# Tile 0's values without half of the row copies, and a new order of the lead-in

## The chip, the cores and the metric

The kernel runs on one core of one Trainium2 chip. The metric is device time in microseconds (us) of one execution. A core has TensorE (PE in the profile, with PEld for its weight loads), VectorE (DVE), ScalarE (ACT), GpSimd (POOL) and SyncE (SP); each takes its own instructions strictly in the order in which the program gives them.

## The reference: what is computed

Causal attention in a window of 64 keys for 8 batches of 8 heads (576 positions, 64 dimensions a head), then a feed-forward layer with g = h * cos(h) on the 4608 rows:

```python
batch, n_heads, seq, head_dim = (8, 8, 576, 64)
...
scores = scale * np.matmul(q, k.transpose(0, 1, 3, 2))
mask = (rel >= 0) & (rel < window)              # window = 64
scores = np.where(mask, scores, -1000000000.0)
attn = np.exp(scores - max) / sum               # softmax by rows
attn_out = np.matmul(attn, v)                   # (B, H, S, D)
x = attn_out.transpose(0, 2, 1, 3).reshape(B * S, H * D)    # 4608 x 512
h = x @ w_in                                    # 512 -> 2048
g = h * np.cos(h)
out = g @ w_out                                 # 2048 -> 512
```

## The kernel before

**Tiles.** The 4608 rows of x are done in 9 tiles of 512 rows, `mt` 0 to 8. A tile's hidden layer has 16 blocks `ff` of 128 columns; each block is the sum of four matmuls, one for each pair of heads (`ks` or `p`, 0 to 3; `first`, L348), 64 matmuls in a tile. ACT then makes the sine, DVE the product gT, and PE the output rows from gT and `w_out` (L534). While a tile's feed-forward layer runs, the attention of the next batch runs in its gaps, by a plan of times (`at`, `pump`).

**Attention units.** A unit (b, p, j) is a batch, a pair of heads and 64 queries; its window is 128 keys, those of block j-1 and block j. Tile 0 needs 32 units, taken as 8 groups of four: group `p.g` has pair p and units 4g to 4g+3. For each group:

- `s` scores (PE, first a matmul that puts in the mask, then eight of 64x64), `m` maximum by rows (DVE), `e` exponentials with their sums (ACT, four), `i` reciprocal of the sums (DVE), `n` norm (POOL or DVE: weights w), `w` transpose on PE into a PSUM tile `tw_ps`, `c` copy of it to SBUF (`g_put`: DVE or ACT, tile wT).
- For each pair: `v` values (16 matmuls over 8 units and 2 heads into o_ps), `x` copy of o_ps to xT (`put_x`), the input of the hidden layer.

Before them stand `tq`, `tk` (transposes of the rows of q and k) and `pq`, `pk` (their copies out of PSUM, tile T).

**The values' rows.** V of batch 0 is loaded in chunks of 128 rows into slots 0, 2, 4, 6 of a tile with 8 slots (`values_of(0)`); the last 64 rows go into the lower half of slot 7 (`load_v`). A unit with odd j finds its 128 keys in slot j-1 as loaded. One with even j needs two halves of different chunks, so `spread_v` makes them: step `z.0` copies the lower 64 partitions of slots 2, 4, 6 to slots 1, 3, 5, and `z.1` the upper 64 partitions of slots 0, 2, 4, 6 to slots 1, 3, 5, 7. Then unit j finds its keys in slot j-1.

**The order of the lead-in.** All that happens before tile 0's hidden layer is written by hand in the string `FIRST`: each word is a step, with pair, group or half, and at the end the engine (a ACT, d DVE, p POOL). `h.p` are first hidden-layer matmuls, for pair p of the first blocks (`skewed`: blocks 0 to 2 before the change); `hx.ff` are those of block ff for pairs 0 and 1, `hl` the matmuls of pairs 2 and 3 of the skewed blocks (5 before the change), `tb` loads the sine's table on ACT. `l` issues the next of seven loads on POOL, in this order: three parts of w_in, q and k of batch 1, two halves of w_out. After `FIRST` POOL issues the last rows of v of batch 0 and the v of batch 1. SP issues only the first two loads in the lead-in.

**PSUM.** The banks O0, O1, X0, X1 and S are handed out by name (`H_FIRST` for the blocks of tile 0, `S_FIRST` for the scores of the lead-in); three more are taken in turn (`ps_t`, tag "t": the transposes and, before the change, all of tile 0's values). A tile waits until the one before it in its place has been read.

Of the kernel before, what the change touches and what calls it, by code (L numbers as in the profile page):

```python
# [10 lines left out]
def _safe_warn(msg, *a, **kw):  # L11
# [4 lines left out]
BF16 = mybir.dt.bfloat16  # L16
AF = mybir.ActivationFunctionType
ALU = mybir.AluOpType
# [7 lines left out]
GF = 4  # L26
# [9 lines left out]
SKEW = 3  # L36
# [3 lines left out]

FIRST = (
# [6 lines left out]
)  # L48


# [1 line left out]
def kernel(  # L52
# [9 lines left out]
    nc = tc.nc  # L62
    B, H, S, D = q.shape
    assert (B, H, S, D) == (8, 8, 576, 64)
    scale = 1.0 / math.sqrt(D)
    d_model = H * D
# [3 lines left out]
    TU = MT // 64  # L70
# [4 lines left out]
    att = ctx.enter_context(tc.tile_pool(name="att", bufs=3))  # L75
# [16 lines left out]
    st = {}  # L92

    H_FIRST = ("O1", "X0", "X1", "S", "O0") * 3 + ("X0",)
    H_SECOND = ("X0", "X1", "S", "O0", "O1") * 3 + ("t",)
    H_BANKS = ("X0", "O0", "X1", "S", "O1") * 2 + ("X0", "X1", "S", "O0", "O1", "t")
    S_BANKS = ("X1", "S", "X0")
# [3 lines left out]
    def bank(which, name):  # L103
        if which == "t":
            return ps_t.tile([128, 512], F32, tag="t", name=name)
        return ps.tile([128, 512], F32, tag=which, name=name)

    def copy(engine, out, in_):
        {"a": nc.scalar.copy, "p": nc.gpsimd.tensor_copy}.get(engine, nc.vector.tensor_copy)(out, in_)  # L109
# [46 lines left out]
    def values_of(b):  # L156
        return rowtiles[0][:, 0:8 * d_model].rearrange("p (s x) -> p s x", s=8) if b == B - 1 else vtiles[b % 3]

    def load_v(b, c):
        n = 128 if c < 4 else 64  # L160
        vt = values_of(b)[:n, 2 * c if c < 4 else 2 * c - 1]
        nc.gpsimd.dma_start(out=vt.rearrange("p (h d) -> p h d", h=H),  # L162
                            in_=v[b, :, c * 128:c * 128 + n, :].rearrange("h p d -> p h d"))


    def spread_v(b, half, engine="p"):
        vt = values_of(b)
        to, of = ((vt[0:64, 1:7:2], vt[0:64, 2:8:2]), (vt[64:128, 1:8:2], vt[64:128, 0:7:2]))[half]
        if engine == "dma":
            nc.sync.dma_start(out=to, in_=of)  # L170
        else:
            copy(engine, to, of)

    def load_w_in(lo, hi):
        nc.gpsimd.dma_start(out=w_in_sb[:, :, lo:hi], in_=w_in_v[:, :, lo:hi])
# [122 lines left out]
    def g_norm(n, engine="p"):  # L298
# [4 lines left out]
                                in1=rden[:, 0:u].unsqueeze(2).to_broadcast([128, u, 128]))  # L303
        st["w", n] = w

    def g_trans(n):
        w, u = st.pop(("w", n)), len(groups[n])
        if n in direct:
            st["tw", n] = t_ps = ps_t.tile([128, GF, 128], BF16, tag="t", name="tw_ps")
            for i in range(u):  # L310
                nc.tensor.transpose(t_ps[:, i], w[:, i], ident)  # L311
            return
        wT = att.tile([128, GF, 128], BF16, tag="wT", name="wT", bufs=20)
        nc.sync.dma_start(out=wT[:, 0:u], in_=w[:, 0:u].rearrange("p u c -> p (u c)"), transpose=True)
        st.update({("wT", unit): wT[:, i] for i, unit in enumerate(groups[n])})

    def g_put(n, engine=None):
        wT, u = att.tile([128, GF, 128], BF16, tag="wT", name="wT", bufs=20), len(groups[n])
        copy(engine, wT[:, 0:u], st.pop(("tw", n))[:, 0:u])
        st.update({("wT", unit): wT[:, i] for i, unit in enumerate(groups[n])})  # L320


    def values(mt, p):
        st["o", mt, p] = o_ps = bank("S", "o_ps") if mt > 1 and p == PAIRS - 1 else ps_t.tile([128, MT], F32, tag="t", name="o_ps")
        for i in range(TU):
            b, j = divmod(mt * TU + i, NU)
            wT = st["wT", (b, p, j)]
            cross = st["cross", (b, p, j)]
            for h in range(2):
                nc.tensor.matmul(out=o_ps[64 * h:64 * h + 64, 64 * i:64 * i + 64],  # L330
                                 lhsT=values_of(b)[:, max(j - 1, 0), 128 * p + 64 * h:128 * p + 64 * h + 64],
                                 rhs=wT[:, 64 * (h ^ cross):64 * (h ^ cross) + 64], start=True, stop=True, skip_group_check=True)


    def put_x(mt, p, engine=None):
        if ("xT", mt) not in st:
            st["xT", mt] = att.tile([128, PAIRS, MT], BF16, tag="xT", name="xT", bufs=2)
        o_ps = st.pop(("o", mt, p))
        copy(engine, st["xT", mt][:, p], o_ps)
# [8 lines left out]
    def first(mt, ff, ks, start, stop):  # L348
        if start:
            st["h", ff] = bank((H_FIRST, H_SECOND, H_BANKS)[min(mt, 2)][ff], "h_ps")  # L350
        nc.tensor.matmul(out=st["h", ff], lhsT=w_in_sb[:, ks, ff * 128:ff * 128 + 128],  # L351
                         rhs=st["xT", mt][:, ks], start=start, stop=stop)

    def skew(mt):
        return 5 if mt < 2 else SKEW

    def last_pairs(mt):
        for ff in range(skew(mt)):
            for ks in range(2, PAIRS):
                first(mt, ff, ks, False, ks == PAIRS - 1)  # L360

    def skewed(mt, ks, n):
        for ff in range(skew(mt) if mt else SKEW):
            first(mt, ff, ks, n == 0, n == PAIRS - 1)

    def last_rows(gT, o_sb):
# [27 lines left out]
    n = n_first  # L394
# [79 lines left out]
    def load():  # L474
# [6 lines left out]
             "pk": lambda p, engine="a": put("k", 0, p, engine),  # L481
             "mk": put_masks, "ck": lambda: cast("k", "d"), "l": load, "tb": sine_table, "h": lambda p: skewed(0, p, next(turn_h)), "hl": lambda: last_pairs(0),
             "hx": lambda ff: [first(0, ff, ks, ks == 0, False) for ks in range(2)],
             "z": lambda half, engine=None: spread_v(0, half, engine),
             "s": lambda p, g: g_scores(2 * p + g, next(turn_s) % 5), "m": lambda p, g: g_max(2 * p + g),
             "e": lambda p, g: g_exp(2 * p + g), "i": lambda p, g: g_inv(2 * p + g),
             "n": lambda p, g, engine: g_norm(2 * p + g, engine), "w": lambda p, g: g_trans(2 * p + g),
             "c": lambda p, g, engine=None: g_put(2 * p + g, engine), "v": lambda p: values(0, p),
             "x": lambda p, engine=None: put_x(0, p, engine)}
    for step in FIRST.split():  # L490
        name, *args = step.split(".")
        steps[name](*[int(a) if a.isdigit() else a for a in args])
    load_v(0, 4)
    for c in range(5):
        load_v(1, c)

    for mt in range(n_mt):
# [11 lines left out]
        for ff in range(n_ff):  # L509
# [8 lines left out]
            e = ff % 2  # L518
# [58 lines left out]
```

## Time and profile before

| what | before |
|---|---|
| median of 3 runs | 306.64 us (305.22 to 307.27) |
| profiled execution, its own time | 306.41 us |
| its span | 304.4 us |
| mean granted clock of TensorE | 0.993 |
| PE busy in the span | 288.7 us |
| DVE, ACT, POOL busy | 220.4, 235.7, 171.1 us |
| HBM read, written | 36.70 MB, 9.44 MB |

The span runs from the first to the last instruction in the trace. A row of the timeline gives start, duration, engine, line, operation, output and inputs, shape and count; in square brackets the idle time before it and what ended it. Durations of successive instructions of one engine overlap by some hundredths of a us, so what one costs is better read from the start of the next. The line of a copy is that of the helper `copy` (L109).

### The profile page before, as it was taken

Reading aid. Unit: us, or ns where it says so; the run is one execution under the profiler, and the core shown is the slowest. Engines: PE = TensorE matmul, PEld = TensorE weight load, DVE = VectorE, ACT = ScalarE, POOL = GpSimd, SP = SyncE. Lnnn points to the kernel's source line nnn. Section 1 sums busy time; section 2 is a strip of 40 time slices with the busy share of each in tenths; the row PEclk is TensorE's granted clock in tenths of the full one; section 3 lists DMA queues with packets and bytes.
Section 4 is the critical chain, followed back from the end, with each engine's and each line's share of the span. In section 5 each row is a group of like instructions: output and inputs, shape, how many; then the busy total and the mean of one; then the engine's idle time right before and its main releaser. Section 6 shows DMA issues by size and latency. Waiting matters only on the chain.

```text
span 304.4 us, 7847 instructions
## 1 busy us (share of the span) xinstructions
PE 288.7 (95%) x2628; PEld 142.1 (47%) x2668; DVE 220.4 (72%) x834; ACT 235.7 (77%) x786; POOL 171.1 (56%) x198
## 2 busy tenths in 40 slices
PE   3769999999999999999999999999999999999996
PEld 3544444544454445444544444444444454454443
DVE  3896889588787878787877787778778877236701
ACT  5997799967997799779987998799869986106600
POOL 8996257977774976497659665967433630000000
PEclk9989999999999999999999999999999999999999
DMA  7999999699969999999999979999994441011012
GB/s 150 181 211 207 207 155 139 105 165 191 225 114 155 225 164 132 154 201 183 138 167 208 189 106 172 157 219 123 180 172 110 87 130 62 0 72 70 0 69 71
DMA packets 165577, 43.88 MB, mean 144 GB/s; under 512 B 154720, under 2 KB 160800, under 8 KB 165536
## 3 DMA queue, kind: packets, MB, share of 16 engines
q0 software_dynamic: 99344, 18.06, 75.1%
q1 hardware_dynamic: 66048, 25.11, 40.2%
q8 instruction: 21, 0.34, 0.5%
q14 instruction: 20, 0.16, 0.2%
q10 hardware_dynamic: 144, 0.20, 0.2%
HBM read 36.70 MB, written 9.44 MB: 152 GB/s over the span
## 4 chain that ended last, share of the span: by engine, by line
PE 88%; DVE 6%; issue 2%; ACT 2%; DMA 1%; POOL 0%; DVEq 0%; POOLq 0%
PE h_ps L351 41%; PE out_ps L534 36%; PE o_ps L330 3%; PE s_ps L261 3%; DVE negm L273 1%; PE out_ps L371 1%; DMA first_f<-in_q_dram 1%; DVE w L302 1%; PE tq_ps L186 1%; DVE s L277 1%; DVE v L109 1%; PE tk_ps L186 1%; PE tw_ps L311 1%; PE s_ps L244 1%; ACT e L288 1%
## 5 line engine op out<-in xcount | busy, mean ns | idle before, releaser
L351 PE MATMUL h_ps<-xT,w_in 128*128 128x512 bf16 x556 | 127.1, 381 | 2.2 <-DVE xT L109 0.6
L534 PE MATMUL out_ps<-w_out,gT 128*128 128x512 bf16 x543 | 123.0, 379 | 1.8 <-issue 1.1
L522 DVE TENSOR_TENSOR gT<-h_ps,sin 128x512 bf16<-128x512 f32 x144 | 95.4, 688 | 33.6 <-ACT sin L519 33.4
L519 ACT ACTIVATE sin<-h_ps 128x512 f32<-128x512 f32 x144 | 82.9, 599 | 34.1 <-PE h_ps L351 32.8
L288 ACT ACTIVATE e<-s,negm 128x128 f32<-128x128 f32 x256 | 98.6, 388 | 0.3 <-DVE negm L277 0.3
L302 POOL TENSOR_TENSOR w<-e,rden 128x512 bf16<-128x512 f32 (+1 forms) x76 | 74.5, 993 | 31.5 <-DVE rden L295 29.1
L351 PEld LDWEIGHTS <-w_in 128*128 128x128 bf16 x576 | 56.0, 98 | 67.1 <-issue 2.7
L534 PEld LDWEIGHTS <-gT 128*128 128x128 bf16 x560 | 53.2, 98 | 62.4 <-issue 0.2
L277 DVE CUSTOM_DVE_ANT_0 s<-s_ps,mask 128x128 f32<-128x128 f32 x256 | 58.0, 284 | 0.1
L288 ACT ACTIVATION_READ_ACCUMULATOR e<-s,negm 128x1 f32 x256 | 48.1, 188 | 0.0
L149 POOL DMA_DIRECT2D rows<-in_q_dram x30 | 25.4, 867 | 25.9 <-DMA T<-rows 16.6
L162 POOL DMA_DIRECT2D v<-in_v_dram x35 | 29.8, 879 | 10.5 <-DMA rows<-in_k_dram 7.3
L109 ACT COPY out_sb<-out_ps 128x512 f32<-128x512 f32 (+1 forms) x18 | 10.1, 563 | 24.2 <-PE out_ps L534 18.7
L295 DVE RECIPROCAL rden<-den 128x4 f32<-128x4 f32 (+1 forms) x80 | 13.8, 172 | 19.2 <-ACT e L288 18.6
L149 POOL DMA_DIRECT2D rows<-in_k_dram x30 | 25.5, 897 | 2.2 <-DMA T<-rows 2.2
L109 DVE CAST xT<-o_ps 128x512 bf16<-128x512 f32 x27 | 17.6, 679 | 6.5 <-PE o_ps L330 6.3
L277 DVE DVE_READ_ACCUMULATOR2_ANT negm<- 128x1 f32 x256 | 21.2, 83 | 0.0
L109 DVE COPY out_sb<-out_ps 128x512 f32<-128x512 f32 x18 | 12.4, 689 | 12.0 <-PE out_ps L534 12.0
L288 ACT ACTIVATE e<-s_ps,negm 128x128 f32<-128x128 f32 x32 | 11.5, 425 | 1.6 <-DVE negm L273 1.6
L261 PE MATMUL s_ps<-T 64*64 64x128 bf16 x512 | 12.1, 221 | 0.0
L261 PEld LDWEIGHTS <-T 64*64 64x64 bf16 x512 | 8.2, 106 | 8.3 <-DVE negm L277 4.4
L330 PEld LDWEIGHTS <-v 128*64 128x64 bf16 x504 | 9.5, 112 | 4.3 <-issue 2.1
(56 smaller groups left out, 146.2 us busy)
## 6 DMA issues: line engine op xcount, KB each, us to landing
out_dram<-out_sb SPq DMA_DIRECT2D x16, 512.0 KB, 6.1
v<-in_v_dram POOLq DMA_DIRECT2D x28, 128.0 KB, 8.3
rows<-in_q_dram POOLq DMA_DIRECT2D x24, 128.0 KB, 5.2
rows<-in_k_dram POOLq DMA_DIRECT2D x24, 128.0 KB, 7.8
w_out<-in_moe_w_out_dram POOLq DMA_DIRECT2D x2, 1024.0 KB, 16.7
w_in<-in_moe_w_in_dram POOLq DMA_DIRECT2D x2, 768.0 KB, 12.4
wT<-w SPq DMA_TRANSPOSE x66, 3.9
out_dram<-out_sb SPq DMA_DIRECT2D x3, 256.0 KB, 2.0
```

The costliest lines, as they stand in the source:

```text
L109: {"a": nc.scalar.copy, "p": nc.gpsimd.tensor_copy}.get(engine, nc.vector.tensor_copy)(out, in_)
L149: nc.gpsimd.dma_start(out=rows(b)[lo:lo + n, slot * 512:slot * 512 + 512].rearrange("p (h d) -> p h d", h=H), in_={"q": q, "k": k}[name][b ...
L162: nc.gpsimd.dma_start(out=vt.rearrange("p (h d) -> p h d", h=H), in_=v[b, :, c * 128:c * 128 + n, :].rearrange("h p d -> p h d"))
L261: nc.tensor.matmul(out=s_ps[cross][to, u].rearrange("p (a t) -> p a t", a=2), lhsT=q_cols(b, p, j)[d], rhs=k_cols(b, p, j)[d], start=True, ...
L277: nc.vector.tensor_tensor_reduce(out=s[:, u], in0=s_ps[:, u], in1=mask[:, 2 - j % 2 if j else 0], scale=-scale if b else -1.0, scalar=BIG, ...
L288: nc.scalar.activation(e[:, u], s[:, u], AF.Exp, bias=negm[:, u:u + 1], scale=1.0 if n < n_first else -1.0, accum_out=den[:, u:u + 1])
L302: (nc.gpsimd if engine == "p" else nc.vector).tensor_tensor(out=w[:, 0:u], in0=e[:, 0:u], op=ALU.mult, in1=rden[:, 0:u].unsqueeze(2).to_br ...
L330: nc.tensor.matmul(out=o_ps[64 * h:64 * h + 64, 64 * i:64 * i + 64], lhsT=values_of(b)[:, max(j - 1, 0), 128 * p + 64 * h:128 * p + 64 * h ...
L351: nc.tensor.matmul(out=st["h", ff], lhsT=w_in_sb[:, ks, ff * 128:ff * 128 + 128], rhs=st["xT", mt][:, ks], start=start, stop=stop)
L519: nc.scalar.activation(sin, h_ps, AF.Sin, bias=math.pi / 2.0)
L522: nc.vector.tensor_tensor(out=gt[:, e], in0=h_ps, in1=sin, op=ALU.mult)
L534: nc.tensor.matmul(out=o_ps[e], lhsT=gT[ff // 2][:, ff % 2, ms * 128:ms * 128 + 128], rhs=w_out_sb[:, ff], start=ff == 0, stop=ff == n_ff - 1)
```

## The change

It does these things:

- Pairs 0 and 1 of tile 0 get their values from v as loaded (`values_first`): for even j, a matmul over the lower 64 rows (part `a`, slot j) and one over the upper 64 rows (part `b`, slot j-2), added in PSUM; odd j as before. They stand in the banks X0 and S.
- The shifted rows are copied only for columns 256 to 511 (pairs 2 and 3), `spread_pairs`; `spread_last` copies the one further half slot that unit 8 of pairs 0 and 1 needs later, behind the loads.
- The norm of the last group of tile 0 is split: three units on DVE, one on POOL (`nh.3.1`). The norm n.1.0 goes from DVE to POOL.
- The order of `FIRST` is new, with some copies on other engines: pk.3, c.1.0 and c.2.0 from ACT to DVE, x.0 from DVE to ACT. Two w_in loads come behind n.0.1; the loads of q and k of batch 1 and of w_out come behind the last norm.
- Fewer hidden-layer matmuls lead: h.0 and h.1 do two blocks instead of three, then hx.2; `hl` finishes three blocks instead of five. `H_FIRST` has another order.

```diff
 FIRST = (
     "tq.0 mk ck tk.0 pq.0.d pk.0.a s.0.1 tq.1 tk.1 l s.0.0 m.0.1 pq.1.d tq.2 e.0.1 pk.1.d s.1.0 pq.2.a "
-    "tk.2 s.1.1 i.0.1 tq.3 l m.0.0 m.1.0 pk.2.d n.0.1.p s.2.0 l w.0.1 tk.3 s.2.1 e.0.0 l e.1.0 m.1.1 "
-    "l i.0.0 e.1.1 pq.3.d i.1.0 m.2.0 pk.3.a e.2.0 n.0.0.p n.1.0.d z.1.p w.0.0 i.1.1 m.2.1 e.2.1 "
-    "s.3.0 s.3.1 c.0.1.d n.1.1.p c.0.0.d w.1.0 m.3.0 i.2.0 z.0.d c.1.0.a n.2.0.p w.1.1 c.1.1.d v.0 "
-    "i.2.1 v.1 n.2.1.p m.3.1 e.3.0 e.3.1 l x.0.d w.2.0 i.3.0 x.1.d h.0 c.2.0.a n.3.0.p w.2.1 h.1 hx.3 "
-    "i.3.1 n.3.1.d w.3.0 c.2.1.a w.3.1 tb v.2 c.3.0.d x.2.a c.3.1.d v.3 l x.3.d hx.4 hl "
+    "tk.2 s.1.1 i.0.1 tq.3 n.0.1.p l l m.0.0 m.1.0 pk.2.d s.2.0 w.0.1 tk.3 s.2.1 e.0.0 e.1.0 m.1.1 "
+    "i.0.0 n.0.0.p e.1.1 pq.3.d i.1.0 n.1.0.p z.1 m.2.0 pk.3.d e.2.0 w.0.0 i.1.1 n.1.1.p m.2.1 e.2.1 "
+    "c.0.1.d s.3.0 s.3.1 z.0 i.2.0 n.2.0.p m.3.0 e.3.0 c.0.0.d w.1.0 va.0 i.2.1 n.2.1.p m.3.1 e.3.1 w.1.1 "
+    "c.1.0.d i.3.0 n.3.0.p c.1.1.d w.2.0 w.2.1 c.2.0.d va.1 vb.0 i.3.1 nh.3.1 l l l l x.0.a c.2.1.a w.3.0 "
+    "c.3.0.d w.3.1 c.3.1.d h.0 vb.1 x.1.d v.2 x.2.a v.3 h.1 hx.2 x.3.d tb hl "
 )
...
-    H_FIRST = ("O1", "X0", "X1", "S", "O0") * 3 + ("X0",)
+    H_FIRST = ("O1", "X0", "O0", "S", "X1") * 2 + ("O1", "X0", "X1", "S", "O0", "X0")
...
+    def spread_pairs(half):
+        vt = values_of(0)[:, :, d_model // 2:]
+        if half:
+            nc.gpsimd.tensor_copy(vt[64:128, 1:8:2], vt[64:128, 0:7:2])
+        else:
+            nc.vector.tensor_copy(vt[0:64, 1:7:2], vt[0:64, 2:8:2])
+
+    def spread_last():
+        vt = values_of(0)[:, :, 0:d_model // 2]
+        nc.gpsimd.tensor_copy(vt[64:128, 7], vt[64:128, 6])
...
+    def g_norm_halves(n):
+        (e, _), rden = st.pop(("e", n)), st.pop(("r", n))
+        w = att.tile([128, GF, 128], BF16, tag="w", name="w", bufs=8)
+        for engine, lo, hi in ((nc.vector, 0, 3), (nc.gpsimd, 3, 4)):
+            engine.tensor_tensor(out=w[:, lo:hi], in0=e[:, lo:hi], op=ALU.mult,
+                                 in1=rden[:, lo:hi].unsqueeze(2).to_broadcast([128, hi - lo, 128]))
+        st["w", n] = w
...
+    def values_first(p, part):
+        if part == "a":
+            st["o", 0, p] = bank(("X0", "S")[p], "o_ps")
+        lower, upper, both = slice(0, 64), slice(64, 128), slice(0, 128)
+        parts = {"a": [(lower, j, j) for j in range(0, TU, 2)] + [(both, j - 1, j) for j in range(1, TU, 2)],
+                 "b": [(upper, max(j - 2, 0), j) for j in range(0, TU, 2)]}[part]
+        for i, (ks, slot, j) in enumerate(parts):
+            for h in range(2):
+                nc.tensor.matmul(out=st["o", 0, p][64 * h:64 * h + 64, 64 * j:64 * j + 64],
+                                 lhsT=values_of(0)[ks, slot, 128 * p + 64 * h:128 * p + 64 * h + 64],
+                                 rhs=st["wT", (0, p, j)][ks, 64 * h:64 * h + 64],
+                                 start=part == "a" and i == 0, stop=True, skip_group_check=True)
...
     def skew(mt):
-        return 5 if mt < 2 else SKEW
+        return 5 if mt == 1 else SKEW
...
-        for ff in range(skew(mt) if mt else SKEW):
+        for ff in range(skew(mt) if mt else 2):
             first(mt, ff, ks, n == 0, n == PAIRS - 1)
...
     load_v(0, 4)
+    spread_last()
```

More of the change, by code (lines that the diff above doesn't have):

```diff
@@ L483 @@
              "hx": lambda ff: [first(0, ff, ks, ks == 0, False) for ks in range(2)],
-             "z": lambda half, engine=None: spread_v(0, half, engine),
+             "nh": lambda p, g: g_norm_halves(2 * p + g),
              "s": lambda p, g: g_scores(2 * p + g, next(turn_s) % 5), "m": lambda p, g: g_max(2 * p + g),
@@ L487 @@
              "n": lambda p, g, engine: g_norm(2 * p + g, engine), "w": lambda p, g: g_trans(2 * p + g),
-             "c": lambda p, g, engine=None: g_put(2 * p + g, engine), "v": lambda p: values(0, p),
+             "c": lambda p, g, engine=None: g_put(2 * p + g, engine), "va": lambda p: values_first(p, "a"), "vb": lambda p: values_first(p, "b"), "v": lambda p: values(0, p),
+             "z": spread_pairs,
              "x": lambda p, engine=None: put_x(0, p, engine)}
```

## The prediction

> **What bounds the kernel now.** I read the page's busy row, then the windows of the lead-in (the stretch before TensorE works without a break), the chain that ended last, and the timeline of each engine there.
>
> ```profile
> PE 288.7 (95%) x2628; PEld 142.1 (47%) x2668; DVE 220.4 (72%) x834; ACT 235.7 (77%) x786; POOL 171.1 (56%) x198
> ```
>
> TensorE (PE) is busy for 288.7 of 304.4 us, so a reordering can only win part of 15.7 us. The next rows are windows: PE, PE weight loads, DVE, ACT and POOL busy us with their counts, then the granted clock, the DMA share and GB/s.
>
> ```profile
> 13.42:16.83 3.41, 2.25 (x34) 1.35 (x34) 3.41 (x8) 3.41 (x20) 3.35 (x3) 1.00 1.23 208
> 16.83:20.24 3.41, 1.68 (x42) 1.22 (x41) 3.41 (x7) 3.23 (x18) 3.33 (x4) 1.00 1.16 211
> 20.24:23.66 3.42, 2.85 (x10) 1.41 (x11) 2.43 (x5) 2.92 (x11) 3.40 (x5) 0.50 1.17 211
> 23.66:27.07 3.41, 3.21 (x49) 1.98 (x49) 1.45 (x3) 1.81 (x4) 3.04 (x4) 1.00 1.21 207
> ```
>
> From 13.4 to 20.2 us DVE, ACT and POOL are all full while PE waits for them. From 20.24 to 23.66 PE has work, but its granted clock is 0.50. The chain shows where this ends.
>
> ```profile
> 17.50 1.41 DVE v L109
> ...
> 22.46 1.73 PE h_ps L351 x5
> ...
> 25.58 0.16 issue
> 25.74 0.59 PE h_ps L351 x2
> ...
> 64.09 9.66 PE h_ps L351 x44
> ```
>
> The DVE copy that spreads the values stands on the chain, then slow hidden-layer matmuls (0.35 us each, against 9.66/44 = 0.22 later). At 25.74 PE starts the run that no longer waits for attention: 8 of tile 0's 64 hidden-layer matmuls are done, 56 remain. What matters is when that point comes and how many matmuls remain.
>
> **ACT.** The changed order gives ACT neither the last key copy (pk.3) nor the copy c.1.0 between its exponentials.
>
> ```profile
> 14.12 0.43 ACT L288 ACTIVATE e<-s_ps,negm 128x128 f32<-128x128 f32 x1
> ...
> 14.47 0.71 ACT L109 COPY T<-tk_ps 128x576 bf16<-128x576 bf16 x1
> 14.99 0.46 ACT L288 ACTIVATE e<-s_ps,negm 128x128 f32<-128x128 f32 x1
> ...
> 17.73 0.72 ACT L109 COPY wT<-tw_ps 128x512 bf16<-128x512 bf16 x1
> 18.20 0.53 ACT L288 ACTIVATE e<-s_ps,negm 128x128 f32<-128x128 f32 x1
> ...
> 21.08 0.37 ACT L288 ACTIVATE e<-s_ps,negm 128x128 f32<-128x128 f32 x1
> ```
>
> Exponentials follow each other every 0.343 us (18.20 less 14.99, less the 0.47 from 17.73 to 18.20, over eight), 1.37 for a group of four. Without the copies (0.52 and 0.47 by start times) and without the wait before the last group (0.48: seven steps from 18.20 end at 20.60, not 21.08), e.2.0 runs from 14.47, e.2.1 from 15.84, e.3.0 from 17.21, e.3.1 from 18.58 to 19.95; the last one starts at 19.61 instead of 21.08. This holds if DVE delivers the maxima in time.
>
> **DVE.** It loses the norm n.1.0, half of the copy z.0 and a quarter of the last norm, and takes pk.3, c.1.0 and c.2.0; x.0 goes to ACT.
>
> ```profile
> 11.22 0.75 DVE L109 COPY T<-tk_ps 128x576 bf16<-128x576 bf16 x1
> ...
> 13.38 0.66 DVE L273 TENSOR_REDUCE negm<-s_ps 128x4 f32<-128x512 f32 x1
> 13.96 1.53 DVE L302 TENSOR_TENSOR w<-e,rden 128x512 bf16<-128x512 f32 x1
> ...
> 16.08 0.74 DVE L109 COPY wT<-tw_ps 128x512 bf16<-128x512 bf16 x2
> ...
> 17.43 1.48 DVE L109 COPY v<-v 64x1536 bf16<-64x1536 bf16 x1
> ...
> 21.57 0.18 DVE L295 RECIPROCAL rden<-den 128x4 f32<-128x4 f32 x1 [0.37 <-ACT e L288]
> 21.79 1.29 DVE L302 TENSOR_TENSOR w<-e,rden 128x512 bf16<-128x512 f32 x1
> ...
> 44.42 0.69 DVE L302 TENSOR_TENSOR w<-e,rden 128x512 bf16<-128x512 f32 x1
> ```
>
> By start spacing a maximum takes 0.58, a reciprocal 0.09, a copy of wT 0.34. From 13.96: pk.3 0.75 to 14.71; i.1.1; m.2.1 to 15.38; c.0.1 to 15.72; z.0, half the elements, 0.74 to 16.46; i.2.0; m.3.0 to 17.13; c.0.0 to 17.47; i.2.1; m.3.1 to 18.14; c.1.0 to 18.48; i.3.0 when e.3.0 is summed, about 18.75; c.1.1 and c.2.0 to 19.5. Every maximum precedes its exponential (m.3.0 by 0.08 us only, the tightest). The last reciprocal came 0.49 after the last exponential started: 20.10. The halved z.0 lies between 0.37 (half its size at twice the speed) and 1.48 (if its time is fixed); I take 0.74, in proportion. At 1.48, m.3.0 and so e.3.0 come 0.66 late, and all behind them.
>
> **The last norm** is split 3:1 over DVE and POOL at once. Its DVE part is 0.52 (three quarters of the undisturbed 0.69) to 1.15 (three quarters of 1.53, beside POOL's norm and copy). I take 0.80, because POOL's quarter overlaps only its first part. It ends at about 21.0, where the old one ended at 23.08.
>
> The Trainium skill (GPSIMD Engine Reference, 1. Specifications) says that POOL shares its SBUF interface with VectorE and contends with DVE instructions that have two SBUF inputs, which speaks against such a split. The three rows agree (0.69, 1.29, 1.53); by the rule at its worst the part takes 1.15 and the sum below is 0.35 worse.
>
> **POOL.** It takes n.1.0, loses half of z.1, and gives its DMA issues another place: the second and third w_in load go behind n.0.1; q, k of batch 1 and both w_out go behind the last norm.
>
> ```profile
> 11.58 0.81 POOL L175 DMA_DIRECT2D w_in<-in_moe_w_in_dram  x1
> 12.38 0.75 POOL L142 DMA_DIRECT2D rows<-in_q_dram  x1
> 13.11 0.76 POOL L142 DMA_DIRECT2D rows<-in_k_dram  x1
> 13.87 1.07 POOL L302 TENSOR_TENSOR w<-e,rden 128x512 bf16<-128x512 f32 x1
> 15.00 2.25 POOL L109 COPY v<-v 64x2048 bf16<-64x2048 bf16 x1
> 17.33 3.22 POOL L302 TENSOR_TENSOR w<-e,rden 128x512 bf16<-128x512 f32 x3
> ```
>
> The w_in issues end at 12.4 as before, so n.0.0 starts when its reciprocal is ready, about 12.7, not 13.87. At 1.05 a norm: n.0.0 to 13.75, n.1.0 to 14.8, z.1 1.13 to 15.93, n.1.1 to 17.0, n.2.0 to 18.05, n.2.1 to 19.1, n.3.0 to 20.15. POOL is thus full, but done as the last reciprocal comes. `spread_last` goes behind all these issues and costs nothing on the path; its reader is the next tile.
>
> **The moved loads.** Each has a landing time, from its issue, in the DMA rows:
>
> ```profile
> w_in<-in_moe_w_in_dram POOLq DMA_DIRECT2D x1, 768.0 KB, 13.4
> rows<-in_q_dram POOLq DMA_DIRECT2D x1, 576.0 KB, 15.4
> rows<-in_k_dram POOLq DMA_DIRECT2D x1, 576.0 KB, 17.5
> ```
>
> They landed at 25.0, 27.8 and 30.6: 2.8 us apart at 205 GB/s, the rate of the windows, in order of issue. So the 15 us are waiting behind w_in. Issued from about 20.6 on, with w_in still in flight until 25, q and k should land as before. PE wants them for its transposes:
>
> ```profile
> 30.98 0.48 PE L186 MATMUL tq_ps<-ident,rows 64*64 64x64 bf16 x36
> ...
> 33.22 0.22 PE L186 MATMUL tk_ps<-ident,rows 64*64 64x64 bf16 x2
> ```
>
> One us earlier, that leaves 2.1 us for q and 1.6 for k; the order of the loads stays, so w_out is unchanged too. I charge nothing; without the cover a hole in the queue costs what exceeds 1.6 us.
>
> **PE.** Values of pairs 0 and 1 take 24 matmuls each instead of 16, eight of them in `vb`.
>
> ```profile
> 13.44 0.41 PE L244 MATMUL s_ps<-T 64*64 64x128 bf16 x8 [0.25 <-issue]
> ...
> 18.42 0.40 PE L311 MATMUL tw_ps<-ident,w 128*128 128x128 bf16 x4 [1.49 <-POOL w L302]
> 18.75 0.90 PE L330 MATMUL o_ps<-wT,v 128*64 128x64 bf16 x32
> ```
>
> Matmuls with 64 rows and 64 columns of values aren't in the trace. Bounds: 13 ns each as the 36 transposes above (0.48), 51 ns as the scores with twice the columns (0.41/8); I take 28 as the o_ps (0.90/32), their nearest kin. The pair 0 work and va.1 lie before 20.3, in PE's waiting time; on the path is only vb.1, 0.22 (0.10 to 0.41), and 0.1 for a change of array shape (0 to 0.25, the issue gap above). From the norm's end at 21.05: w.3.1 0.33, h.0 (two matmuls) 0.44, vb.1 0.32, v.2 and v.3 0.45 each, h.1 0.44, hx.2 0.44: 23.92. The copies x.1 (about 22.9) and x.3 (about 23.8) are in time. I add the 0.16 of issue that the old kernel had there and 0.16 for waits that such a replay misses: hl starts at 24.24.
>
> **The sum.** 25.74 less 24.24 is 1.50 earlier. But six hidden-layer matmuls are done then, not eight: 0.44 back. Net 1.06, and nothing behind should absorb it: PE sets the pace there. The order of PSUM banks changes for ff 2 and 4 and their reuse, and only ff 9 to ff 12 comes closer, with two whole ffs (1.7 us) between. The profiled execution took 306.41 (2.0 around its span), 0.23 under the median of the runs: 305.35 by it, 305.58 by the median. **I predict 305.5.**
>
> **Rivals.**
> *The clock falls again.* The window with 2.25 us of PE work was followed by full clock, that with 1.68 by 0.50. My replay gives 2.4 from 16.83 to 20.24, hardly more, and part of it is 64-row work. If it falls, the 2.6 us of PE work before 23.66 lose 1.3: 306.8, no change. The Trainium skill (TensorE: Matmul & The Clock Gate, Part 1: The HAM clock gate) lets the clock fall only after an idle window of about 3.4 us; the trace has the length (3.42) but not the idleness. By that rule the new kernel stays at full clock, 305.5; the page's statement that the window runs freely also means that runs can differ, for which the runs of before (305.22 to 307.27) leave room.
> *POOL becomes the bound.* If z.1 at half size still takes 2.25, n.3.0 ends at 21.27 and the last norm 1.1 later: 306.6; with z.0 fixed as well 307.2. For it: POOL has no slack. Against: an elementwise copy of half the columns.
> *The loads come late (slower).* If 15.4 us is what that load takes after its issue, q lands at 36.0 when PE wants it at 29.9: 6.1 lost, 305.35 + 6.1 = 311.5. It decides from q later than 29.9 or k later than 32.2. Against: landings spaced by bytes.
> *More than forecast.* The norm at 0.52, no added waits, vb at 13 ns: 304.7; with DVE and ACT freed of contention as well, 303.3 or less.
>
> **How the numbers follow.** Forecast 0.52, clock 0.20, POOL 0.12, late loads 0.09, more 0.07. A measurement tells about 1% (3.1 us) from no change. Faster by that: only "more", 0.07. Slower: late loads and 0.02 of POOL's tail, 0.11. The rest, 0.82, is within 1%. The forecast's own range is 304.7 to 306.2 (vb and the norm at their ends, the waits); with the clock, POOL and the spread of the runs, 303.8 to 307.5.
>
> **What would show it.** Last exponential of e.3.1 starting near 19.6; n.3.0 ending near 20.2; the split norm's DVE part 0.5 to 1.15; granted clock 1.00 from 20.2 to 23.7; tile 0's third and later pair sums starting near 24.2; q and k of batch 1 landing near 27.8 and 30.6. It is wrong if PE waits at the batch-1 transposes, if maxima come after their exponentials' turn, or if PE loses later what it won here.

## The result: slower, and the profile after

| what | before | after |
|---|---|---|
| median in the comparison | 305.96 us (305.22 to 307.27) | 309.31 us (308.97 to 311.33) |
| ratio after to before, 95% interval | | 1.0108 (1.0076 to 1.0139) |
| profiled execution, its span | 306.41, 304.4 us | 308.97, 306.8 us |
| mean granted clock | 0.993 | 0.988 |

The changed kernel is 3.3 us slower; 305.5 was forecast, with a range up to 307.5. The busy row, the clock in 40 slices of 7.67 us and the shares of the chain that ended last, from the page of after:

```profile
PE 290.0 (95%) x2645; PEld 143.1 (47%) x2684; DVE 219.1 (71%) x835; ACT 234.9 (77%) x784; POOL 171.6 (56%) x201
...
PEclk9977999999999999999999999999999999999999
...
PE 68%; DMA 14%; ACT 6%; POOL 5%; issue 4%; DVE 3%; POOLq 0%; DVEq 0%
```

and the last of these of before:

```profile
PE 88%; DVE 6%; issue 2%; ACT 2%; DMA 1%; POOL 0%; DVEq 0%; POOLq 0%
```

PE is still busy for 95% of the span, but of the chain it now holds 68% instead of 88%, and DMA 14% instead of 1%: at some places PE waits for a transfer where it did not. The clock is low in the third and fourth slices, 15 to 31 us.

**The engines in the lead-in** (timeline of after; start, duration, instruction) do what the replay said:

```profile
15.43 0.56 DVE L179 COPY v<-v 64x768 bf16<-64x768 bf16 x1
15.79 4.12 POOL L313 TENSOR_TENSOR w<-e,rden 128x512 bf16<-128x512 f32 x4
...
19.36 0.53 ACT L299 ACTIVATE e<-s_ps,negm 128x128 f32<-128x128 f32 x1
...
20.23 0.56 DVE L321 TENSOR_TENSOR w<-e,rden 128x384 bf16<-128x384 f32 x1
20.27 0.77 POOL L321 TENSOR_TENSOR w<-e,rden 128x128 bf16<-128x128 f32 x1 [0.36 <-DVE rden L306]
```

The last exponential starts at 19.36 (19.61 in the replay), POOL's four norms end at 19.91 (20.15), the split norm at 21.04 (21.0). Up to here the change is worth what was forecast.

**PE** then does this (timeline of after):

```profile
20.16 1.29 PE L330 MATMUL tw_ps<-ident,w 128*128 128x128 bf16 x8
21.25 1.06 PE L383 MATMUL h_ps<-xT,w_in 128*128 128x512 bf16 x2
22.23 0.42 PE L362 MATMUL o_ps<-wT,v 64*64 64x64 bf16 x8
22.59 1.07 PE L349 MATMUL o_ps<-wT,v 128*64 128x64 bf16 x32
23.59 0.61 PE L383 MATMUL h_ps<-xT,w_in 128*128 128x512 bf16 x1
24.41 7.11 PE L383 MATMUL h_ps<-xT,w_in 128*128 128x512 bf16 x28 [0.22 <-issue]
31.45 0.48 PE L197 MATMUL tq_ps<-ident,rows 64*64 64x64 bf16 x36
```

From 21.25 to 23.59 pass 2.34 us; the replay had 0.44 + 0.32 + 0.90 = 1.66 for the same work. The batch-1 transposes `tq` are a fixed place in PE's order: they start at 31.45, where before had 30.98. A gain of 1.06 was forecast there, so 1.53 are already missing. The windows of after (PE, weight loads, DVE, ACT, POOL busy us with counts, granted clock, DMA share, GB/s), first cut where the prediction cut those of before, then where the clock changes:

```profile
16.83:20.24 3.41, 2.52 (x53) 1.97 (x54) 2.24 (x9) 3.15 (x19) 3.04 (x4) 0.88 1.16 209
...
12.58:16.00 3.42, 2.57 (x44) 1.57 (x37) 3.22 (x10) 3.42 (x22) 3.14 (x4) 1.00 1.48 199
16.00:19.41 3.41, 1.69 (x36) 1.31 (x36) 2.85 (x9) 3.41 (x23) 3.37 (x4) 1.00 1.16 211
19.41:22.83 3.42, 3.35 (x52) 1.99 (x46) 1.74 (x6) 1.65 (x6) 3.06 (x5) 0.50 1.15 210
22.83:26.24 3.41, 3.19 (x38) 1.69 (x34) 1.25 (x2) 2.07 (x3) 3.37 (x5) 0.50 1.08 164
```

The forecast's 2.4 us of PE work between 16.83 and 20.24 are there (2.52). But this execution's clock does not change at 20.24; it falls at 19.41 and rises at 26.24. The stretch of one window's length before 19.41 holds only 1.69 us of PE work, almost the 1.68 that lay before the fall in the kernel before. And the half clock lasts two such lengths, 6.83 us, because the 3.35 us of work in the first of them, small matmuls for the most part, did not raise it. The second, with 3.19 us and more large matmuls (128x512) in it, did. Before, 2.85 us in six large matmuls and four of 128x128 did at once.

**The loads.** DMA rates in 40 slices of 0.725 us from 18 to 47 us, and issues with their us to landing; after, then before:

```profile
GB/s 208 206 206 235 203 208 193 126 153 174 184 186 161 205 215 180 161 193 204 202 209 206 209 195 208 205 208 208 209 204 195 161 163 158 155 154 153 109 77 137
...
rows<-in_q_dram POOLq DMA_DIRECT2D x1, 576.0 KB, 7.8
rows<-in_k_dram POOLq DMA_DIRECT2D x1, 576.0 KB, 10.1
```

```profile
GB/s 237 191 208 206 213 218 204 202 208 213 205 210 205 204 207 204 208 213 208 205 232 189 201 212 205 208 206 204 182 161 170 149 155 154 151 137 139 139 152 162
```

From the eighth slice (23.1 us) on there is a hole: 126 to 186 GB/s where before had 202 to 213. q and k, issued at 20.99 and 21.79, land at 28.8 and 31.9, 1.0 and 1.3 us later than before, and w_out at 37.5 and 43.1, 1.8 and 2.4 later.

**Later on** PE has three waits for POOL or a transfer between 30 and 125 us; before had none (timeline of after):

```profile
50.88 0.34 PE L330 MATMUL tw_ps<-ident,w 128*128 128x128 bf16 x3 [0.63 <-POOL w L313]
...
75.07 0.64 PE L272 MATMUL s_ps<-T 64*64 64x128 bf16 x32 [0.31 <-DMA T<-rows]
...
121.24 1.12 PE L349 MATMUL o_ps<-wT,v 128*64 128x64 bf16 x46
123.38 0.47 PE L349 MATMUL o_ps<-wT,v 128*64 128x64 bf16 x18 [1.02 <-DMA wT<-w]
```

How far the same work starts behind that of before, by start times in the two timelines:

| work | before | after | behind |
|---|---|---|---|
| tq of batch 1 | 30.98 | 31.45 | 0.47 |
| values at 57 us | 57.37 | 58.38 | 1.01 |
| values at 120 us | 120.08 | 121.24 | 1.16 |
| values at 151 us | 150.95 | 153.22 | 2.27 |
| the last values, at 266 us | 266.45 | 268.84 | 2.39 |

So half of the loss is there by the values at 120 us; the other half comes in one step, at the wait for a transposed block (wT) at 123 us, which nothing in the change touches.

### The profile page after: what moved, and what is told of

It reads as the page before. It is cut to its first block, busy times and chain, and to the rows that moved or that the text cites. A ratio compares the mean times of both kernels' runs of the same rounds, so it can differ in the third digit from the quotient of the medians.

```text
span 306.8 us, 7887 instructions
## 1 busy us (share of the span) xinstructions
PE 290.0 (95%) x2645; PEld 143.1 (47%) x2684; DVE 219.1 (71%) x835; ACT 234.9 (77%) x784; POOL 171.6 (56%) x201
## 4 chain that ended last, share of the span: by engine, by line
PE 68%; DMA 14%; ACT 6%; POOL 5%; issue 4%; DVE 3%; POOLq 0%; DVEq 0%
PE h_ps L383 32%; PE out_ps L568 29%; DMA w_out<-in_moe_w_out_dram 6%; ACT e L299 4%; DMA rows<-in_k_dram 3%; PE s_ps L272 3%; DMA T<-rows 2%; POOL w L313 2%; PE o_ps L349 2%; DMA wT<-w 1%; POOL rows L149 1%; PE out_ps L403 1%; DVE s L288 1%; DMA first_f<-in_q_dram 1%; PE tq_ps L197 1%
## 5 line engine op out<-in xcount | busy, mean ns | idle before, releaser
L109 ACT COPY out_sb<-out_ps 128x512 f32<-128x512 f32 (+1 forms) x18 | 10.2, 566 | 24.6 <-PE out_ps L568 19.1
L109 DVE CAST xT<-o_ps 128x512 bf16<-128x512 f32 x26 | 16.9, 680 | 8.6 <-PE o_ps L349 7.6
L349 PE MATMUL o_ps<-wT,v 128*64 128x64 bf16 x472 | 10.5, 200 | 1.1 <-DMA wT<-w 1.0
```

## The experiments

Three causes had to be told apart: the **clock**, the **late loads**, and, once the first runs had shown the wait at 123 us in different kernels, PE's **instruction fetch**. Ratios are to the kernel before, run on the same chip in the same job.

### The loads alone, in the kernel before (e1)

The four issues are moved behind the last norm, as in the change; nothing else.

```diff
-  "... e.0.0 l e.1.0 m.1.1 l i.0.0 ... e.3.1 l x.0.d ... i.3.1 n.3.1.d w.3.0 ... v.3 l x.3.d hx.4 hl "
+  "... e.0.0 e.1.0 m.1.1 i.0.0 ... e.3.1 x.0.d ... i.3.1 n.3.1.d l l l l w.3.0 ... v.3 x.3.d hx.4 hl "
```

> The kernel before, with one thing of the change: q and k of batch 1 and both w_out are issued behind the last norm (n.3.1), as the changed kernel does. Theory D (the late issue leaves a hole in the DMA queue at 23 to 27 us; all later loads land 1 to 2.4 us late, and the later tiles wait for them): landings of batch 1's q and k near 28.8 and 31.9, v of batch 1 spread near 47 instead of 44.7, and the time 1.5 to 2 us above before, about 307.5, although POOL is freed of 3.4 us of issue in the lead-in. Theory C (only the half clock in the lead-in costs): no slower than before, 305 to 306.2.

Measured: 307.22 us (before 306.08), ratio 1.0031 (1.0013 to 1.0050). The move lets POOL norm earlier: the last norm that is POOL's in the lead-in (n.3.0) starts at 20.28 instead of 21.46, and tq at 29.07, 1.9 earlier than in before. Not all of the 1.9 is the move's: the traced execution is the one of ten that kept full clock, and before's trace has half clock from 20.24 to 23.66. But the rate falls to 119 GB/s at 23 us, POOL's issues of v stand until q and k have landed, and PE waits for a norm on POOL:

```profile
49.53 0.34 PE L311 MATMUL tw_ps<-ident,w 128*128 128x128 bf16 x3 [1.67 <-POOL w L302]
```

At the values at 57 us (57.04) 0.33 of the 1.9 are left. By the medians the move is not free, and this lead at 29 us isn't kept.

### The changed kernel with q earlier, with full clock, with both (e2, e3, e4)

e2 issues q of batch 1 behind n.2.1, so that the queue does not run dry. e3 puts seven idle 128x512 matmuls into PE's waiting time (five before va.0, two before w.2.1), to keep the clock. e4 does both.

```diff
-  "... n.2.1.p m.3.1 ... nh.3.1 l l l l x.0.a ..."
+  "... n.2.1.p l m.3.1 ... nh.3.1 l l l x.0.a ..."          # e2, e4
-  "... w.1.0 va.0 ... w.2.0 w.2.1 ..."
+  "... w.1.0 k.5 va.0 ... w.2.0 k.2 w.2.1 ..."              # e3, e4
+    def idle_matmuls(n):
...
+        for _ in range(n):
+            nc.tensor.matmul(out=st["idle"], lhsT=ident, rhs=mask16[:, 0:4].rearrange("p u c -> p (u c)"),
+                             start=True, stop=True, skip_group_check=True)
```

> The changed kernel with one of the four late loads (q of batch 1) issued three us earlier, behind the norm n.2.1. POOL is full there, so the last norm comes about 0.4 us later. Theory D: 2.8 us of transfer more in the queue closes the hole; v of batch 1 is spread near 45, and the time falls by 1.5 to 2, less 0.4, to about 307.8. Theory C: the 0.4 is lost, about 309.7.

> The changed kernel with seven idle matmuls of 128x512 (mask by identity into the bank X1, never read) where TensorE waits in the lead-in: five before va.0, two before w.2.1. Both theories: the granted clock stays 1.00, and tile 0's uninterrupted run starts about 1.5 us earlier, so that PE reaches the batch-1 transposes near 30 instead of 31.45. Theory C: the whole 1.5 us shows, 307.8. Theory D: the loads are late as before, so PE waits longer for them in the later tiles and the time falls by 0.5 at most, 308.8 or more.

> Both edits together: q of batch 1 behind n.2.1, and the seven idle matmuls. Theory D with C (two costs that add): the forecast of the prediction comes back, 305.4 to 306.2, below before or level with it. If it stays above 307, a third cost is missing from both theories.

| kernel | us | ratio |
|---|---|---|
| e2 q early | 308.39 | 1.0086 (1.0056 to 1.0116) |
| e3 full clock | 307.13 | 1.0046 (1.0029 to 1.0063) |
| e4 both | 306.91 | 1.0030 (1.0006 to 1.0053) |

e2 fills the hole (at least 196 GB/s in every slice up to 39 us), and its interval overlaps that of after: the loads explain little. e4 lost full clock in three of its ten executions in spite of the idle matmuls. In e3 the clock is 1.00 in all ten executions, and the gain against the 1.0108 of after is 0.6%, some 1.9 us (not all of it the clock's: see e10 and e13). The windows of e3 and PE's rows:

```profile
16.00:19.41 3.41, 3.30 (x44) 1.79 (x42) 2.79 (x10) 3.41 (x22) 3.14 (x4) 1.00 1.16 211
19.41:22.83 3.42, 2.87 (x74) 1.92 (x70) 2.31 (x6) 2.01 (x9) 3.06 (x5) 1.00 1.13 203
...
29.60 0.48 PE L197 MATMUL tq_ps<-ident,rows 64*64 64x64 bf16 x36
...
120.77 1.10 PE L349 MATMUL o_ps<-wT,v 128*64 128x64 bf16 x50 [0.68 <-DMA wT<-w]
```

At full clock tq starts at 29.60; the prediction's sum says 30.98 less 1.06, 29.92. The sum up to there was right for a chip that keeps its clock. Yet e3 is still slower than before: the lead of 1.38 is given back, part of it at a wait for wT. That wait is in e4 too (0.97), and in e2 (0.93 and 0.63).

### Is the wait for wT made by other transfers? (e5, e6)

The loads of v for batches 3 to 6, which share the DMA engines with the transposes, are left out, in before (e5) and in after (e6).

```diff
-            at(t0 + (0.5 if b == 2 else 14) + 0.8 * c, load_v, b, c)
+            if b == 2 or b == B - 1:
+                at(t0 + (0.5 if b == 2 else 14) + 0.8 * c, load_v, b, c)
```

> The kernel before, with the loads of v of batches 3 to 6 left out (their tiles keep older values): 2.6 MB less through POOL's queue, and 20 DMA issues less on POOL ahead of the norms of the later tiles. It is the base for the next run. All theories: before shows no DMA wait of PE in the later tiles, so the time stays within 0.5 us of before, 305.5 to 306.2.

> The changed kernel with the same loads left out. Theory L (of the 3.3 us, about 0.5 to 1 is lost up to the end of tile 0, and the rest where PE waits in tile 4 for weights whose norm stands on POOL behind loads that wait for landings): the wait at 121 to 124 us goes, and the kernel lies 1.0 to 1.3 above the run before this one, about 307. Theory C (the half clock in the lead-in costs all of it): the distance stays near 3, 309.

e5: 305.84 us, ratio 0.9979 (0.9949 to 1.0009); e6: 307.88, 1.0057 (1.0036 to 1.0077). The distance between them is 2.0 us (3.3 with the loads; the intervals are too wide to say that it shrank). The wait of after is still in e6, 1.50 long, so those loads don't make it. What the queue did then (e6, the issues of tile wT with min, median and max us to landing):

```profile
DMA to landing us min/median/max: 2.4/2.4/4.7
```

Four of the six transposes land 2.4 us after their issue, the first 2.9 and the last 4.7, with no load beside it. In that stretch another queue has an entry: q8, kind "instruction". It carries 0.34 MB in 21 packets, 16 KB each; PE's 2645 matmuls and 2684 weight loads in after are 5329 instructions, and 0.34 MB over them is 64 bytes each. So these are PE's instructions, in blocks of 256, and where in the program a block is fetched depends on how many instructions stand ahead of it. After has 33 more recorded PE instructions than before. The entry in after, and in before:

```profile
q8 instruction: 1, 0.02, 7.7%
```

```profile
q8 instruction: 1, 0.02, 5.9%
```

The first is of the window 120 to 121 us (after), the second of 123 to 124 us (before; its values start at 120.08 and are over by then). The rates in 40 slices of 0.05 us, after from 119 to 121 and from 121 to 123, then before from 121 to 123:

```profile
GB/s 189 225 230 189 210 236 164 246 220 195 190 68 11 0 0 0 0 0 0 0 0 0 0 328 5 67 133 200 205 210 205 220 195 210 215 174 195 128 67 16
...
GB/s 5 0 0 0 0 0 0 0 10 179 10 5 10 15 5 10 10 10 10 5 15 5 10 15 11 0 0 0 36 56 133 236 220 200 230 195 200 246 189 195
```

```profile
GB/s 230 241 179 230 220 179 205 230 200 210 236 179 220 230 210 230 225 200 230 220 215 210 230 205 230 215 210 220 225 195 236 215 210 210 230 195 205 236 205 200
```

The single 328 is 16 KB in 0.05 us, the block, at 120.15. Behind it the queue moves some 10 GB/s from 121 to 122.4, while PE's last values wait. Before has no such trickle in this stretch.

### The values alone (e7), three of the loads late (e8), 32 more instructions (e9)

e7 is before with the values in halves and half of the row copies, in the old order. e8 is e1 with q issued behind n.2.1. e9 is before with 16 small matmuls at its start, each with its weight load, 32 PE instructions that no later step reads.

```diff
-  "... n.1.0.d z.1.p ... i.2.0 z.0.d ... c.1.1.d v.0 i.2.1 v.1 ... e.3.0 e.3.1 ... h.0 ..."
+  "... n.1.0.d z.1 ... i.2.0 z.0 va.0 ... c.1.1.d i.2.1 ... e.3.0 va.1 vb.0 e.3.1 ... h.0 vb.1 ..."   # e7
-  "... n.2.1.p m.3.1 ... n.3.1.d l l l l w.3.0 ..."
+  "... n.2.1.p l m.3.1 ... n.3.1.d l l l w.3.0 ..."        # e8, against e1
+    pad_ps = bank("X1", "pad_ps")                           # e9
+    for _ in range(16):
+        nc.tensor.matmul(out=pad_ps[0:64, 0:64], lhsT=ident[:, 0:64], rhs=ident[:, 0:64],
+                         start=True, stop=True, skip_group_check=True)
```

> The kernel before, with the values part alone: row-split matmuls for pairs 0 and 1 in the banks X0 and S, half of the row copies, the order, the norms, the loads and the lead of hidden-layer matmuls as before (va and vb stand where v.0 and v.1 stood). If this part pays as the prediction reckoned (1.1 us less POOL, 0.9 less DVE in the lead-in), the time is 0.3 to 0.8 below before, 305.3 to 305.8. If its 64-row matmuls lower the granted clock at a time that counts, it is 0.5 to 1.5 above before.

> The kernel before with k of batch 1 and both w_out behind the last norm, and q behind n.2.1. Between 23 and 27 us the DMA queue should not run dry (over 200 GB/s). Theory D (late landing cost e1 its lead): PE keeps the 1 to 1.9 us that it won in e1's lead-in, the time is 305, below before. If the lead goes again between 41 and 57 us with the loads on time, something else sets that stage, and the time is 306 or more.

> The kernel before with 32 more instructions on PE and nothing else: 16 pairs of weight load and 128x64 matmul on the identity into the bank X1, never read, ahead of tq.0, where PE has nothing to do until 4.4 us. The change adds 32 PE instructions too. Theory F (PE's instructions come by DMA in blocks of 256; the block that is fetched at 123 us in before, behind tile 4's values, comes some 4 us earlier with 32 more ahead of it and holds up the last DMA transpose of the weights that these values wait for): a fetch at 118 to 120 us, a PE wait of 0.7 to 1.5 us on wT near 121 to 123, and 0.7 to 1.5 us more than before, 307. Theory V (the wait belongs to the values part in some other way): no wait there, 306.1.

| kernel | us | ratio |
|---|---|---|
| e7 values alone | 311.07 | 1.0162 (1.0135 to 1.0189) |
| e8 three loads late | 305.80 | 0.9992 (0.9972 to 1.0013) |
| e9 32 more PE instructions | 307.72 | 1.0047 (1.0026 to 1.0068) |

**e9 is the decisive run.** Nothing of the work differs from before, the values at 120 us start 0.19 later, the block is now fetched between 120 and 121, and the wait is there, where before had none:

```profile
120.27 1.12 PE L330 MATMUL o_ps<-wT,v 128*64 128x64 bf16 x46
122.95 0.47 PE L330 MATMUL o_ps<-wT,v 128*64 128x64 bf16 x18 [1.55 <-DMA wT<-w]
```

It costs 1.6 us by the medians. The transposes' landings fit: the last of the six before these values lands 4.3 to 4.9 us after its issue in the five traces whose block is fetched while it is under way (after, e2, e6, e7, e9), and 2.4 us in the seven whose block comes behind it (before, e1, e5, e8, e12, e15, e16). **e7** is slower than the whole change. Its clock:

```profile
13.14:16.55 3.41, 1.50 (x22) 0.78 (x20) 2.90 (x8) 3.41 (x20) 3.27 (x5) 0.93 1.30 205
16.55:19.97 3.42, 2.73 (x33) 1.79 (x33) 1.90 (x6) 3.10 (x17) 2.08 (x3) 0.50 1.16 212
19.97:23.38 3.41, 3.02 (x31) 1.57 (x30) 1.21 (x3) 2.07 (x10) 3.10 (x4) 0.50 1.17 210
23.38:26.79 3.41, 3.16 (x23) 1.70 (x23) 1.47 (x3) 2.07 (x3) 3.37 (x5) 0.57 1.20 206
```

Half clock for 10.2 us, three window lengths (16.10 to 26.34), and the wait for wT behind it (1.42 at 125.15). **e8** shows that the late loads cost little when the queue is kept filled: in the traced execution, one of two in ten that kept full clock, the lead of 1.98 at tq (29.00) is 1.26 at the values at 57 us (56.11) and 1.3 in the span (303.1 against 304.4). The median is that of before.

### Fetch moved, and the causes taken away together (e10 to e16)

e10 is after with 24 small matmuls at its start (48 instructions, so that the block falls elsewhere). e11 is e4 with them, against all three causes at once (three of its ten executions still lose full clock). e12 is e8 with six idle matmuls for the clock. e13 is e3 with the 24, so with clock and fetch removed and the loads left late; e14 is e7 with the 24 and eight idle matmuls. e15 is e12 with k behind n.2.1 too; e16 is e15 without idle matmuls.

```diff
+    for _ in range(24):                                     # e10, e11, e13, e14
+        nc.tensor.matmul(out=pad_ps[0:64, 0:64], lhsT=ident[:, 0:64], rhs=ident[:, 0:64], ...)
-  "... c.0.0.d w.1.0 m.3.0 ... n.2.1.p l m.3.1 ... x.1.d h.0 ... n.3.1.d l l l w.3.0 ..."
+  "... c.0.0.d w.1.0 k.5 m.3.0 ... n.2.1.p l m.3.1 ... x.1.d k.1 h.0 ... n.3.1.d l l l w.3.0 ..."   # e12, against e8
+  "... c.0.0.d w.1.0 k.5 m.3.0 ... n.2.1.p l l m.3.1 ... x.1.d k.1 h.0 ... n.3.1.d l l w.3.0 ..."   # e15
+  "... n.1.0.d z.1 k.5.0 w.0.0 ... e.3.0 k.3.1 va.1 vb.0 ..."                                       # e14, against e7
```

> The changed kernel with 24 such pairs at the same place: 48 more PE instructions, 80 more than before. Theory F: the fetch near 120 comes about 5 us earlier and meets transposes with slack; the wait at 123 us goes, and the time falls by 1.0 to 1.5 to 308. Theory V: the wait stays, 309.3.

> The changed kernel with the three edits: q of batch 1 behind n.2.1, seven idle matmuls of 128x512 in the lead-in, and 24 pairs at the start. If clock, loads and instruction fetch are the whole loss, the wait at 122 is gone and the time is e4 less about 1: 305.5 to 306, level with before or a little below, as the prediction had it for undisturbed clock and loads. If it stays near 307, something is still missing.

> The kernel before with k of batch 1 and both w_out behind the last norm, q behind n.2.1 (as e8), and six idle matmuls of 128x512: five behind w.1.0, one before h.0. All theories: the clock stays 1.00 in every run, and the time is that of e8's runs at full clock, 304.5 to 305.3, below before and after. If the fetch of instructions (12 more) meets tile 4's transposes, 0.5 to 1 more.

> The changed kernel with the seven idle matmuls and the 24 pairs at the start; the loads as late as in the change. If the late loads cost by themselves: 0.6 to 1.3 above e11, 307.5 to 308.2, with PE waiting for POOL's norm near 49. If they only showed because other delays met them: 306.9 like e11.

> e7 (the kernel before with the values part alone) with eight idle matmuls of 128x512 where PE waits (five before w.0.0 in bank O0, three before va.1 in X1) and the 24 pairs at the start. If e7's 4.9 us are clock and fetch alone, the time falls to 305.3 to 306.2, level with before or below; if the values part costs by its own work (16 more matmuls, the later x.0), it stays at 307 or more.

> e12 with k of batch 1 issued early as well, behind q, after n.2.1; only w_out stays behind the last norm. If late landings took back e12's lead between 41 and 57 us, the DMA queue now stays over 200 GB/s from 22 to 28 us, the wait for the norm near 49 falls from 1.44 to under 0.8, and the time is 304.8 to 305.3, below before. If another thing sets that stage: 306.

> The same without idle matmuls (e8 with k early). The clock falls in most runs as in e8: 0.3 to 1 above e15, 305.3 to 306.

| kernel | us | ratio |
|---|---|---|
| e10 after, fetch moved | 307.57 | 1.0053 (1.0030 to 1.0077) |
| e11 after, fetch, clock and q | 306.90 | 1.0027 (1.0005 to 1.0050) |
| e13 after, fetch and clock | 307.18 | 1.0025 (1.0008 to 1.0043) |
| e14 values alone, fetch and clock | 307.59 | 1.0050 (1.0029 to 1.0070) |
| e12 before, three loads late, clock | 305.99 | 0.9997 (0.9972 to 1.0022) |
| e15 before, two loads late, clock | 305.82 | 0.9987 (0.9968 to 1.0007) |
| e16 before, two loads late | 305.87 | 0.9993 (0.9972 to 1.0014) |

In e10 the block is fetched between 118 and 119, two us earlier than in after, with the values at 121.11, and the wait shrinks from 1.02 to 0.35:

```profile
122.59 0.47 PE L349 MATMUL o_ps<-wT,v 128*64 128x64 bf16 x18 [0.35 <-DMA wT<-w]
```

Against after that is 0.55%, 1.7 us, with the clock still low in the lead-in (tq at 31.58). The fetch alone is thus worth about as much as in e9. In e11's trace, which like before's has one stretch of half clock (21.73 to 25.14), PE goes nearly level with before all the way, tq at 30.93 and the values at 151 us at 151.26 (150.95), and no wait for a transfer above 0.16 is left. e13 against e10 adds the clock alone: 0.3%, with intervals that overlap, and the two executions of e10 that kept the clock at 1.00 took 307.47 and 307.65, in the midst of its others (306.66 to 308.83). So the 1.9 of e3 is partly the fetch's: its idle matmuls moved the block as well, to between 117 and 118. e13, with late loads, is no different from e11: once clock and fetch are out of the way, the late loads cost nothing that these runs can tell. In e14 tq stands at 32.23, in an execution with half clock from 21.58 to 25.00 (four of its ten lost some), and the values alone remain 1.5 us slower than before, of their 4.9.

e15 is the best of all; its interval holds 1. At full clock and without a hole it leads before by 1.5 us at the values at 57 us (55.85), and then:

```profile
73.36 0.64 PE L261 MATMUL s_ps<-T 64*64 64x128 bf16 x32 [1.14 <-DMA T<-rows]
```

PE stands until the rows of a later batch have been transposed; 0.56 of the lead is left at 88.64. e12 and e15 kept the clock at 0.998 or more in all ten executions, yet missed the times expected of them. e16 kept it in one of ten; in its trace, with half clock from 18.54 to 25.37, tq starts at 31.91 instead of e15's 29.46, and its median is 0.05 above e15's, not 0.3 or more. A lead of over 2 us at tq was worth nothing at the end here that these runs can tell. No version here beats before by more than the measurement can tell.

## Why the prediction was wrong, step by step

**The replay of ACT, DVE and POOL was right**, within 0.25 us at each of its ends. The copy z.0 took 0.56 (0.74 was taken, "in proportion"), z.1 1.03 (1.13), the DVE part of the norm 0.56 (0.80; the lower end was 0.52). The rival that POOL becomes the bound fell with the 1.03.

**The clock was the first step to fail.** The step "My replay gives 2.4 from 16.83 to 20.24, hardly more" measured the new work in the windows of the old execution. The work came (2.52), but the windows did not stay: here the clock changes at 19.41, where it changed at 20.24 before. As a window may begin anywhere, any stretch of 3.4 us counts, and one with 1.69 was in the plan. The rival "The clock falls again" had the mechanism and gave it 0.20; its price of 1.3 was too small, because it let the clock rise at 23.66, and it rose at 26.24. At tq full clock is worth 1.85 us (31.45 against 29.60 in e3), and the 1.06 forecast there became a loss of 0.47. What it is worth in the total isn't settled: 0.9 by the ratios of e13 and e10, whose intervals overlap, and at most the 1.9 of e3 against after, with a moved fetch.

Nor is lost clock peculiar to the changed kernel. Of the 107 executions of before that ran beside the experiments seven kept clock 1.00 (median 305.15), 40 had 0.993 or 0.994 (306.18) and 58 had 0.987 or 0.989 (306.15), about what three of the four of after had (0.988 and 0.989); those took 308.97 to 309.45, still some 3 us more. How long the clock is low thus doesn't tell the two kernels apart; where it is low may. e5, which is before up to the loads of v left out, had half clock from 16.16 to 22.99 and its tq at 30.74, no later than the 30.98 of before.

The Trainium skill (TensorE: Matmul & The Clock Gate, Part 1: The HAM clock gate) lets the clock fall after an idle window and says that the window runs freely. The trace agrees with the second. With the first it does not: the stretch with 1.69 of 3.41 us busy was followed by half clock, so half-busy is not safe, and the 3.35 us busy stretch behind it did not raise the clock as the page's busy window would. I used the page as an argument for full clock; the measurement decides against it.

**"With w_in still in flight until 25, q and k should land as before"** failed as well. w_in did stay in flight until about 25 with the late loads (24.75 in e1; after's trace lacks that landing), but only its last packets: from 23 to 25 us those of w_in (1536 bytes each) moved 85 KB in after and those of q (1152 bytes) 209 KB, where before moved 42 and 378. A landing at 25 does not say that the queue is full until then, and the hole of 23 to 27 us follows. The consequence was not the one watched for: PE did not wait at tq or tk, but POOL's later issues and so the norm at 50.88 came late. Its price is small: e2 0.9 us by medians, with intervals that overlap, and nothing in e13 against e11.

**A cost that was not in the sum at all** is the third: some 32 more PE instructions move the fetch of a block to the last transposes before the values at 120 us, 100 us behind the edit. e9 shows 1.6 us for it in a kernel that is otherwise before, e10 takes 1.7 off after. That the number of instructions does it is shown; that the block's packet holds up the transposes inside the DMA engines is inferred from the rates and from the landings (4.3 to 4.9 us against 2.4). The six traces whose values near 120 us waited 0.9 us or longer for wT had the block 0.3 to 2.0 us ahead of them; in e3 (2.0 ahead) the wait was 0.68, in e10 (2.9) 0.35, and with the block five us ahead or behind the values at most 0.15.

**"Nothing behind should absorb it"** failed as well. Leads at tq of 1.4 (e3), 1.9 (e1), 1.5 (e15) and 2.0 us (e8), all in traces with full clock, were -0.4, 0.3, 0.5 and 1.3 in the span: they went at norms that stood behind POOL's issues, at transposed rows and, in e3, at the wait for wT. Nor do the costs add: e3 gives back 1.9, e10 1.7 and e2 0.9, 4.5 in sum, where all three edits together give back 0.8%, 2.5 us (e11); that e3 moved the block as well is part of this.

**What stays open.** With all three edits (e11), and with those for clock and fetch alone (e13), the changed kernel is 0.25% slower than before, some 0.8 us. This isn't the clock; at equal clock the rest is larger. Before's seven executions at clock 1.00 have spans of 303.1 to 303.7, the seven of e11 at 0.999 or 1.00 303.8 to 305.1; their medians are 305.15 and 306.67 us, 1.5 apart, and e13's at that clock is 2.0 above. The values in halves alone, with the edits for clock and fetch, cost 1.5 by the medians (e14) and 2.1 at clock 1.00 (six executions, 307.23). So the rest may be theirs, and the 0.22 that the prediction charged for them on the path too little: they take 16 more matmuls, and x.0 comes later. That isn't shown. Which waits carry it to the end wasn't settled; they differ from execution to execution.

## What to carry to other kernels

Place the PE work of a lead-in in every stretch of a clock window's length, wherever it begins, not in the windows of the last profile; and keep each well above two thirds busy, since the clock fell behind up to 2.21 of 3.41 us here (e6), and in e4 in spite of idle matmuls. When a kernel comes out different far from the edit, look at the instruction queue in the DMA rows: adding PE instructions moves the fetches behind them, and a few idle instructions at the start show it in one run. A lead in the first 30 us is worth only what the next wait for a load or a transposed row leaves of it.

## What the hardware showed that I had not expected

- PE's instructions came through the DMA engines in 21 blocks of 16 KB; with one just ahead of it or beside it, a DMA transpose took 4.7 instead of 2.4 us to land.
- In the traced lead-ins, cut into windows of 3.41 us from where the clock changes, a full clock fell behind every window with up to 1.69 us of PE work and held behind every one with 2.24 (e12) or more. Between them it did both: it held behind 1.97 to 2.13 (e1, e8) and fell behind 2.00 to 2.21 (e16, e14, e11, e4, e6). It did not rise behind one with 3.35 us, 1.1 of it in 128x512 matmuls and the rest in smaller ones; it did rise behind one with 2.85 us, most of it in 128x512 matmuls.
- A norm split over DVE and POOL: DVE's three quarters took 0.56, near the 0.52 of undisturbed work, while POOL's quarter took 0.77, where a whole norm there takes 1.03 (4.12 over four). POOL's part ended 0.25 us behind DVE's, a quarter of 1.03, which fits POOL waiting until DVE was done; no run tests that.
